# Minimum before maximum in GpSimd's clamp of the weights' upper words

## The chip, the cores and the metric

The kernel runs on one core of a Trainium2 chip. The metric is device time in microseconds (us) of one execution, lower is better; before the change it is the median of three runs. The profile is of one execution, taken by the hardware profiler. Engines are named as in the profile: PE is TensorE's matmul, PEld its weight load, DVE VectorE, ACT ScalarE, POOL GpSimd, SP the engine that issues the DMAs.

## The reference

Linear attention without softmax, an RMS norm for each head, and a feed-forward layer with SiLU:

```python
def _attn_ref(q, k, v, g_norm):            # 8 batches, 8 heads, 576 tokens, 64 per head
    kv = np.einsum('bhsd,bhse->bhde', k, v)
    out = np.einsum('bhsd,bhde->bhse', q, kv)
    rms = np.sqrt(np.mean(out * out, axis=-1, keepdims=True) + 1e-06)
    return (out / rms * g_norm).astype(np.float32)

def _moe_ref(x, w_in, w_out):              # x: 4608 tokens x 512; w_in: 512 x 2048; w_out: 2048 x 512
    h = x @ w_in
    g = h * (1.0 / (1.0 + np.exp(-h)))
    return (g @ w_out).astype(np.float32)
```

The attention's output, with the heads side by side, is x. The two weight matrices arrive as 64-bit floats.

## The kernel before

**Tiles.** The 4608 tokens are nine tiles of 512 (t = 0 to 8), and the 2048 hidden columns are 16 blocks of 128 (f = 0 to 15). The main loop runs over t and inside it over f. One step (t, f) computes the block's hidden values by `products` (line 428) on PE, the gate by `gate` (line 437), and two steps later the block's share of the output by `project` (line 457). Every operand of these matmuls is kept as an upper and a lower part (xh and xl, gh and gl, and the two halves of a weight block), and three products of parts stand for one. `products` therefore has 12 matmuls in a step and `project` 12. The attention of the later batches is spread over the steps by tables of jobs.

**Weights.** A block of w_in (wi0 to wi15) or of w_out (wo0 to wo15) is 128 x 512 numbers of 64 bits. It is turned into float32 parts once, and then stays in SBUF for all nine tiles. So the conversion of nearly all blocks falls into the first tile, t = 0, whose step f prepares the blocks wi of f + 2 and wo of f, with the clamps of one block further. A few blocks come before, in the startup. For each block:

1. `load_block` (line 105): a DMA of 512 KB from the SP queue; upper and lower 32-bit words lie side by side.
2. `magnitude` (line 118): ACT takes the upper words, read as float32, without their sign into the tile `full` (line 126); GpSimd clamps `full` in place to the limits SMALLEST and LARGEST (line 127). For block wi0 alone both are done on VectorE (lines 122 and 127).
3. `bits` (line 131): three bit operations on VectorE (lines 146, 149 and 152) put the float32 together from `full` and the two words.
4. `split_block` (line 157): ACT rounds to the upper part (line 160), GpSimd subtracts to the lower part (line 161).

In the first tile GpSimd also has the subtraction that makes gl (line 443; in the other tiles it is VectorE's), and the one that makes xl from the attention's output (lines 295 and 399).

**Order.** The program is written under a manual schedule: each engine runs its instructions in the order in which the code issues them. In step f of the first tile this is, for GpSimd, the lower parts of the two blocks prepared in the step before (line 161), the clamps of two further blocks (line 127), the subtraction for gl (line 443), and any xl. A block's bits can't be put together before its clamp, its parts not before its bits, and PE's `products` and `project` wait for the parts. The tiles `full` come from a pool of eight buffers shared with other temporaries; gf (line 439) has one buffer. The loads' order is the list ORDER at the top of the file.

Of the kernel before, what the change touches and what calls it, by code (L numbers as in the profile page):

```python
# [12 lines left out]
ALU = mybir.AluOpType  # L13
# [6 lines left out]
SMALLEST = 2.0 ** -15  # L20
LARGEST = 122879.9921875
# [9 lines left out]
def linear_attention_rms_silu_ffn(  # L31
# [51 lines left out]
    for i in range(4):  # L83
        nc.gpsimd.tensor_copy(
            out=both[32 * i:32 * i + 32, 32 * (i ^ 1):32 * (i ^ 1) + 32], in_=ident[32 * i:32 * i + 32, 32 * i:32 * i + 32]
# [24 lines left out]
    def low_high(kind, f):  # L110
        w = words[kind, f].rearrange("p a b -> p (a b)").rearrange("p (n two) -> p n two", two=2)
        return w[:, :, 0], w[:, :, 1]

    def full_tile(kind, f):
        fulls[kind, f] = t = tmp.tile([P, S], F32, name="full", tag="tmp")[:, :NP * P]
        return t

    def magnitude(kind, f, on_vector=False):

        full, high = full_tile(kind, f), low_high(kind, f)[1]  # L120
        if on_vector:
            nc.vector.tensor_scalar(
                out=full.bitcast(I32), in0=high, scalar1=0x7FFFFFFF, scalar2=None, op0=ALU.bitwise_and
            )
        else:
            nc.scalar.activation(out=full, in_=high.bitcast(F32), func=AF.Abs)  # L126
        (nc.vector if on_vector else nc.gpsimd).tensor_scalar(  # L127
            out=full, in0=full, scalar1=SMALLEST, scalar2=LARGEST, op0=ALU.max, op1=ALU.min
        )

    def bits(kind, f):
# [389 lines left out]
    with tc.manual_schedule():  # L521
# [64 lines left out]
        keep_warm(2)  # L586
        p0.copy_kv()
        magnitude("wi", 0, True)
        w("wi0", 1)
        p0.make_out()  # L590
# [18 lines left out]
        p2.copy_kv()  # L609
        n(p1, 2)  # L610
        magnitude("wi", 1)
        p2.make_out()
        n(p1, 4)
# [13 lines left out]
        n(p2, 4)  # L627
        x(p1, 2)
        magnitude("wi", 2)
        n(p3, 2)  # L630
        p2.make_x()
# [114 lines left out]
```

## Time and profile before

| | |
|---|---|
| median of three runs | 904.36 us (904.27 to 904.51) |
| the profiled execution's own time | 904.43 us |
| its span, first to last instruction | 902.7 us |
| instructions in the span | 11085 |
| mean granted clock of TensorE | 0.996 |
| read from and written to HBM | 45.09 MB, 9.44 MB |

The profile's page gives busy times of each engine, and slices of the span in which a digit is the busy share in tenths. A group of instructions reads: line, engine, operation, output <- inputs, shapes, count, then busy us and mean ns of one, then the idle time of the engine just before them, with what ended it. A row of a timeline reads: start, duration, engine and instruction, then in brackets the idle time before it. A row of waits reads: who waited for whom, us in total, how often, the longest.

The chain of work that ended last lies on PE for 84% of the span, almost all of it in lines 432 and 462, the matmuls of `products` and `project`.

### The profile page before, as it was taken

The page shows a single profiled execution, that of the slowest core. Times are in us where ns is not written, and L with a number is a line of the kernel's source. Part 1 is how long each engine was busy: PE and PEld are TensorE (multiplying, and loading weights), DVE is VectorE, ACT ScalarE, POOL GpSimd, SP SyncE. Part 2 cuts the span into 40 slices and gives each one's busy share as a digit, 9 for nine tenths or more (in the row PEclk, how much of TensorE's full clock was granted, in tenths as well). Part 3 has the DMA queues.
Part 4 walks back from the last instruction along what each step waited for, and adds up shares of the span by engine and source line. Part 5 has one row for each costly group of instructions (what it writes and reads, how often), then busy time and mean ns, then how long its engine had stood idle before and what let it go on. Part 6 is the DMA issues. An engine that isn't in the chain of part 4 may idle for free.

```text
span 902.7 us, 11085 instructions
## 1 busy us (share of the span) xinstructions
PE 878.6 (97%) x4472; PEld 717.3 (79%) x4472; DVE 300.5 (33%) x535; ACT 301.8 (33%) x671; POOL 210.0 (23%) x180
## 2 busy tenths in 40 slices
PE   8899879999999999999999999999999999999998
PEld 8677657888888888888888888888888888888887
DVE  4766683323241324232423224232513141111111
ACT  4656443432243224422432234322432232112112
POOL 2999995200111012101120112001210010000000
PEclk9999999999999999999999999999999999999999
DMA  9549101310032003200221014100300010001001
GB/s 333 230 159 366 51 1 44 122 40 1 1 126 80 0 1 126 67 13 1 91 75 40 1 38 128 40 1 1 126 1 1 1 47 1 1 1 48 1 0 47
DMA packets 23971, 55.24 MB, mean 61 GB/s; under 512 B 2800, under 2 KB 3056, under 8 KB 23920
## 3 DMA queue, kind: packets, MB, share of 16 engines
q1 hardware_dynamic: 23920, 54.54, 17.6%
q8 instruction: 35, 0.57, 0.3%
q14 instruction: 16, 0.13, 0.0%
HBM read 45.09 MB, written 9.44 MB: 60 GB/s over the span
## 4 chain that ended last, share of the span: by engine, by line
PE 84%; POOL 0%; ACT 0%; issue 0%; ACTq 0%
PE hp L432 39%; PE acc L462 39%; PE at L222 2%; PE at L260 1%; PE at L261 1%; PE at L259 1%; PE at L462 1%; PE at L409 0%; PE at L408 0%; POOL xl L295 0%; ACT ob L467 0%; ACTq L467 0%
## 5 line engine op out<-in xcount | busy, mean ns | idle before, releaser
L432 PE MATMUL hp<-xh,wi 128*128 128x512 f32 x1144 | 355.3, 392 | 11.0 <-POOL wi L161 11.0
L462 PE MATMUL acc<-wo,gh 128*128 128x512 f32 (+1 forms) x1152 | 357.4, 392 | 0.1
L432 PEld LDWEIGHTS hp<-xh,wi 128*128 128x128 f32 x1144 | 215.0, 188 | 56.6 <-POOL wi L161 13.9
L443 DVE TENSOR_TENSOR gl<-gf,gh 128x512 fp32r<-128x512 f32 x128 | 88.6, 692 | 503.7 <-ACT gf L442 503.7
L462 PEld LDWEIGHTS acc<-wo,gh 128*128 128x128 f32 x1152 | 215.5, 189 | 44.8 <-POOL wo L161 0.3
L441 ACT ACTIVATE gh<-hp 128x512 fp32r<-128x512 f32 x143 | 85.4, 597 | 437.6 <-PE hp L432 437.4
L432 PE MATMUL hp<-xl,wi 128*128 128x512 f32 x572 | 228.2, 399 | 1.5 <-POOL xl L295 1.5
L462 PE MATMUL acc<-wo,gl 128*128 128x512 f32 x576 | 223.3, 388 | 2.4 <-POOL gl L443 2.4
L295 POOL TENSOR_TENSOR xl<-o,xh 128x448 fp32r<-128x448 f32 (+7 forms) x56 | 52.9, 945 | 345.0 <-ACT xh L294 345.0
L462 PEld LDWEIGHTS acc<-wo,gl 128*128 128x128 f32 x576 | 108.6, 189 | 26.6 <-POOL gl L443 2.8
L432 PEld LDWEIGHTS hp<-xl,wi 128*128 128x128 f32 x572 | 107.7, 188 | 24.5 <-POOL xl L295 1.9
L442 ACT ACTIVATE gf<-hp 128x512 f32<-128x512 f32 x143 | 84.8, 593 | 23.0 <-POOL gl L443 22.9
L246 POOL TENSOR_TENSOR ql<-q,qh 128x576 fp32r<-128x576 f32 x24 | 34.2, 1425 | 173.2 <-ACT qh L245 168.2
L127 POOL TENSOR_SCALAR full<-full 128x512 f32<-128x512 f32 x31 | 58.9, 1910 | 0.9 <-ACT full L126 0.9
L286 DVE SCALAR_TENSOR_TENSOR o<-o,gcol,yT 128x448 f32<-128x448 f32 (+7 forms) x56 | 39.0, 696 | 2.0
L265 ACT ACTIVATE sq<-at 128x288 f32<-128x288 f32 x56 | 23.2, 414 | 42.6 <-PE at L261 35.0
L146 DVE TENSOR_SCALAR conv<-full 128x512 int32<-128x512 int32 x32 | 22.2, 694 | 30.7 <-POOL full L127 29.4
L222 PEld LDWEIGHTS at<-v,k 128*64 128x64 f32 (+1 forms) x560 | 20.8, 136 | 14.3 <-issue 8.9
L229 ACT COPY kvm<-at 64x64 f32<-64x64 f32 x56 | 11.5, 205 | 55.5 <-PE at L222 55.2
L222 PE MATMUL at<-v,k 128*64 128x64 f32 (+1 forms) x560 | 26.5, 231 | 1.9 <-ACT o L266 1.9
L279 DVE STREAM_TRANSPOSE yT<-y 128x448 f32<-128x448 f32 (+7 forms) x56 | 26.3, 470 | 0.1
L294 ACT CAST xh<-o 128x448 fp32r<-128x448 f32 (+7 forms) x56 | 24.7, 441 | 0.0
(95 smaller groups left out, 473.7 us busy)
## 6 DMA issues: line engine op xcount, KB each, us to landing
out<-ob SPq DMA_DIRECT2D x35, 256.0 KB, 2.5
wi<-in_moe_w_in SPq DMA_DIRECT2D x16, 512.0 KB, 8.1
wo<-in_moe_w_out SPq DMA_DIRECT2D x16, 512.0 KB, 9.1
k<-in_k SPq DMA_DIRECT2D x28, 288.0 KB, 2.9
v<-in_v SPq DMA_DIRECT2D x28, 288.0 KB, 3.4
q<-in_q SPq DMA_DIRECT2D x28, 288.0 KB, 2.9
early_wo<-in_k SPq DMA_DIRECT2D x2, 288.0 KB, 4.7
early_wi<-in_v SPq DMA_DIRECT2D x2, 288.0 KB, 4.6
```

What stands on the lines that cost most here:

```text
L127: (nc.vector if on_vector else nc.gpsimd).tensor_scalar(out=full, in0=full, scalar1=SMALLEST, scalar2=LARGEST, op0=ALU.max, op1=ALU.min)
L222: nc.tensor.matmul(out=self.kv[h], lhsT=self.k[rows, c, :], rhs=self.v[rows, c, :], start=(r == 0), stop=(r == 4))
L246: nc.gpsimd.tensor_tensor(out=self.ql, in0=self.q, in1=self.qh.bitcast(F32), op=ALU.subtract)
L279: nc.vector.transpose(out=self.yT.rearrange("p (j a) -> p j a", a=32), in_=y[:, a // 32:e // 32].unsqueeze(2).to_broadcast([P, (e - a) // ...
L286: nc.vector.scalar_tensor_tensor(out=self.o[:, a:e], in0=self.o[:, a:e], scalar=gcol, in1=self.yT, op0=ALU.mult, op1=ALU.mult)
L294: nc.scalar.copy(out=th[:, self.c, w], in_=self.o[:, a:e])
L295: nc.gpsimd.tensor_tensor(out=tl[:, self.c, w], in0=self.o[:, a:e], in1=th[:, self.c, w].bitcast(F32), op=ALU.subtract)
L432: nc.tensor.matmul(out=hp[:, :TN], lhsT=w[:, a, fs], rhs=x[:, c, :], start=(c == 0 and i == 0), stop=(c == NP - 1 and i == 2),)
L441: nc.scalar.activation(out=gh, in_=hp[:, :TN], func=AF.Silu)
L442: nc.scalar.activation(out=gf, in_=hp[:, :TN], func=AF.Silu)
L443: (nc.gpsimd if t == 0 else nc.vector).tensor_tensor(out=gl, in0=gf, in1=gh.bitcast(F32), op=ALU.subtract)
L462: nc.tensor.matmul(out=bank, lhsT=g[:, ns], rhs=w[:, a, cs], start=(f == 0 and i == 0), stop=(f == NF - 1 and i == 2))
```

## The change

In the clamp the minimum with LARGEST is now the first operation and the maximum with SMALLEST the second. Line 127 serves both engines, so the one clamp on VectorE (wi0) is changed along with the 31 on GpSimd. The limits are SMALLEST = 2^-15 and LARGEST = 122879.9921875.

```diff
@@ -125,7 +125,7 @@
         else:
             nc.scalar.activation(out=full, in_=high.bitcast(F32), func=AF.Abs)
         (nc.vector if on_vector else nc.gpsimd).tensor_scalar(
-            out=full, in0=full, scalar1=SMALLEST, scalar2=LARGEST, op0=ALU.max, op1=ALU.min
+            out=full, in0=full, scalar1=LARGEST, scalar2=SMALLEST, op0=ALU.min, op1=ALU.max
         )
```

No instruction is added, removed or moved on any engine, and no wait or DMA changes.

## The prediction

> **What bounds the kernel now.** I read the page's busy table and its slices first, then the GpSimd groups, then windows around the place where the changed line runs, and last the waits.
>
> ```profile
> PE 878.6 (97%) x4472; PEld 717.3 (79%) x4472; DVE 300.5 (33%) x535; ACT 301.8 (33%) x671; POOL 210.0 (23%) x180
> ...
> PE   8899879999999999999999999999999999999998
> ...
> POOL 2999995200111012101120112001210010000000
> ...
> L127 POOL TENSOR_SCALAR full<-full 128x512 f32<-128x512 f32 x31 | 58.9, 1910 | 0.9 <-ACT full L126 0.9
> ```
>
> Over the whole span TensorE (PE) is the bound, at 97%, and GpSimd (POOL) has 23%. The averages hide one stage: in slices 2 to 6 (a slice is 902.7/40 = 22.6 us) POOL stands at 9 while PE falls to 7. All 31 changed GpSimd instructions are there; they are 58.9 of POOL's 210.0 us. The changed line also runs once on VectorE, for block wi0. So I look at the first token tile in windows (us from the span's start; then the length, and the busy time and count of each engine):
>
> ```profile
> 34.60:145.00 110.40, 92.33 (x437) 70.56 (x437) 74.47 (x108) 56.40 (x115) 110.40 (x77) 0.97 0.33 121
> ...
> 79.70:87.30 7.60, 7.60 (x50) 6.01 (x49) 5.67 (x9) 4.71 (x12) 7.60 (x7) 1.00 1.03 408
> 87.30:94.80 7.50, 7.50 (x34) 6.12 (x33) 5.55 (x9) 4.74 (x10) 7.50 (x5) 1.00 0.82 311
> ...
> 109.80:117.30 7.50, 5.76 (x25) 4.42 (x24) 6.85 (x17) 3.44 (x6) 7.50 (x6) 1.00 0.01 2
> ...
> 145.00:241.00 96.00, 96.00 (x494) 78.30 (x493) 28.89 (x56) 31.25 (x74) 12.87 (x13) 1.00 0.16 49
> ```
>
> The fifth busy figure is POOL's: from 34.60 to 145.00 us it is busy for 110.40 of 110.40 us, while PE (the first) has 92.33. In the second token tile, 145.00 to 241.00 us, PE is busy all the time and POOL for 12.87 us. So **GpSimd sets the pace of the first tile, for 110.4 us, and TensorE everything after it.** The waits agree:
>
> ```profile
> PE hp L432 <- POOL wi L161: 11.0, 7, 2.8
> ...
> PE acc L462 <- POOL gl L443: 2.4, 1, 2.4
> ...
> PE hp L432 <- POOL xl L295: 1.5, 1, 1.5
> ...
> DVE conv L146 <- POOL full L127: 29.4, 17, 3.8
> ```
>
> PE waits 14.9 us for POOL (11.0 + 2.4 + 1.5) and VectorE waits 29.4 us for the clamp itself. What follows one clamp is queued in order on POOL, and its last item frees the second tile:
>
> ```profile
> 109.84 1.27 POOL L443 TENSOR_TENSOR gl<-gf,gh 128x512 fp32r<-128x512 f32 x1
> 111.08 1.26 POOL L161 TENSOR_TENSOR wi<-full,wi 128x512 fp32r<-128x512 f32 x1
> 112.31 1.28 POOL L161 TENSOR_TENSOR wo<-full,wo 128x512 fp32r<-128x512 f32 x1
> 113.57 3.79 POOL L127 TENSOR_SCALAR full<-full 128x512 f32<-128x512 f32 x2
> 117.33 1.28 POOL L443 TENSOR_TENSOR gl<-gf,gh 128x512 fp32r<-128x512 f32 x1
> ...
> 143.13 1.12 POOL L295 TENSOR_TENSOR xl<-o,xh 128x448 fp32r<-128x448 f32 x1
> ...
> 144.31 0.50 PE L432 MATMUL hp<-xl,wi 128*128 128x512 f32 x1 [1.49 <-POOL xl L295]
> ```
>
> One step of the tile (one f of 16) is gl, wi, wo and two clamps, from 109.84 to 117.33 us: 7.49 us without a gap, of which the two clamps are 3.79. At its end xl ends at 143.13 + 1.12 = 144.25 us and PE starts at 144.31. So each 0.1 us more on a clamp reaches PE undiminished, and each 0.1 us less does until PE itself is the bound.
>
> **The change, part by part.** It moves nothing: instructions, their order on every engine, waits, buffers and DMAs stay. It exchanges two operations and their two constants within each clamp. The lower limit is below the upper one, so the result is the same for every number, and the later instructions see the same data. Only the duration of the 31 GpSimd instructions and of the one on VectorE can change.
>
> *The one on VectorE (wi0).*
>
> ```profile
> L146 DVE TENSOR_SCALAR conv<-full x32: 682/695/697, 8.1 to 138.3; 128x512 int32<-128x512 int32 x32
> L127 POOL TENSOR_SCALAR full<-full x31: 1904/1909/1922, 17.0 to 136.4; 128x512 f32<-128x512 f32 x31
> ...
> L122 DVE TENSOR_SCALAR full<-wi x1: 427/427/427, 7.2 to 7.2; 128x512 int32<-128x512 int32 x1
> L127 DVE TENSOR_SCALAR full<-full x1: 428/428/428, 7.7 to 7.7; 128x512 f32<-128x512 f32 x1
> ```
>
> The columns behind the name are shortest, median and longest in ns. L122 does one operation in 427 ns, L127 two in 428 ns. The second operation costs VectorE nothing, so which is the second cannot matter: 0 taken. The far end would be the slower VectorE form of the same size, 695 - 428 = 0.27 us, once, and as much less on the other side: ±0.03%, under what counts.
>
> *The 31 on GpSimd.* The trace has no clamp with the minimum first, so its price is bounded. What the rows say of the present form: 31 runs lie between 1904 and 1922 ns, over 31 different blocks and 120 us of differing surroundings. So the time depends neither on the values nor on what runs beside it. How much of it is the loop over elements? Two other sizes give a fixed part and a slope:
>
> ```profile
> 155.55 0.46 POOL L295 TENSOR_TENSOR xl<-o,xh 128x128 fp32r<-128x128 f32 x1 [3.67 <-ACT xh L294]
> ...
> L84 POOL COPY both<-ident 32x32 f32<-32x32 f32 x4 | 0.8, 203 | 0.1
> ...
> L82 POOL COPY both<-ident 128x128 f32<-128x128 f32 x1 | 0.3, 280 | 0.0
> ...
> L161 POOL TENSOR_TENSOR wi<-full,wi 128x512 fp32r<-128x512 f32 x16 | 20.4, 1277 | 12.9 <-ACT wi L160 12.9
> ```
>
> A subtraction of 128 columns takes 460 ns and one of 512 columns 1277 ns: 817/384 = 2.13 ns a column and some 188 ns fixed (an estimate from these two rows). The copies give (280 - 203)/96 = 0.80 ns a column. The clamp, with the same fixed part, has (1909 - 188)/512 = 3.36 ns a column: four times a copy, 1.6 times a subtraction, though it reads only one tensor. So its time is in the arithmetic, not in reading or writing. A maximum and a minimum against a constant are mirror images (compare, then choose); taking 1.68 ns for each gives the same sum in either order. **I take no change, 1909 ns.** The near ends are the fast one of a subtraction, 1281 ns (row of line 443 below), and the slow one of two such passes, one for each operation, 2 x 1281 = 2562 ns. The far ends are a copy of this size, 203 + 480 x 0.80 = 587 ns, and two passes as long as today's, 3818 ns.
>
> [...]
>
> How many of the 31 count? POOL's groups between 34.60 and 145.50 us:
>
> ```profile
> L127 POOL TENSOR_SCALAR full<-full 128x512 f32<-128x512 f32 x27 | 51.2, 1909 | 0.0
> ...
> L443 POOL TENSOR_TENSOR gl<-gf,gh 128x512 fp32r<-128x512 f32 x16 | 20.5, 1281 | 0.0
> ```
>
> 27 clamps lie in the stretch without idle time; the four before it, at 17.0 to 31.1 us, have gaps around them. So the time moves by 27 times the change of one clamp, up to 31 times where it gets slower. At 1909 ns again: 27 x 0 = 0. The profiled execution took 904.43 us around a span of 902.7 us, 0.07 above the median of 904.36 of the three runs; I predict 904.4 us.
>
> **The rivals.** The bound for "faster" or "slower" is 0.2%, 1.8 us, about what a measurement of this kernel can tell from no change; over 27 clamps that is 67 ns on one, 3.5% of it.
>
> *First rival, faster: the new order has a better loop, about as quick as a subtraction (1281 ns).* For it: the clamp is 4 times a copy per column, so there is room. Against it: nothing in a row makes the two orders differ. Price: 27 x (1909 - 1281) = 17.0 us. In the windows from 79.70 to 94.80 us PE has no idle time, so their four clamps (2.5 us) may give nothing: 14.5 to 17.0 us, that is 887 to 890 us, likeliest 889. A loop that gains less gives proportionally less, up to 902.
>
> *Second rival, faster: a loop near the copy's (587 ns).* POOL would save 27 x 1.32 = 35.7 us, more than PE can use, and PE becomes the bound of the first tile. Its floor there:
>
> ```profile
> L462 PE MATMUL acc<-wo,gh 128*128 128x512 f32 x112 | 37.0, 413 | 0.1
> L432 PE MATMUL hp<-xh,wi 128*128 128x512 f32 x112 | 36.8, 411 | 11.0 <-POOL wi L161 11.0
> L432 PE MATMUL hp<-xl,wi 128*128 128x512 f32 x56 | 23.4, 418 | 1.5 <-POOL xl L295 1.5
> L462 PE MATMUL acc<-wo,gl 128*128 128x512 f32 x56 | 22.6, 403 | 2.4 <-POOL gl L443 2.4
> ...
> 145.27 2.79 PE acc L462 x12
> ```
>
> The first four rows are the large matmuls of the stretch, 112 + 112 + 56 + 56 = 336. The chain has twelve in 2.79 us, 0.23 us each at full pace (the mean durations overlap). The second tile, with 16 steps of 24, has 384 in 96 us along with its other work; 48 fewer make 96 - 48 x 0.23 = 85 us, against 110.4 now. So at most 25.4 us go, to 879 us; since the weights' DMAs already run at a share of 1.03 (the column before GB/s, the last) from 79.70 to 87.30 us, some waits will be left, and I put it at 879 to 886, likeliest 883. [...]
>
> *Third rival, slower: the present order is the one with the fused loop, and the other falls back to one pass for each operation.* For it: the row shows the present order alone, which may as well be the better of the two. Against it: 3.36 ns a column, four times a copy, doesn't look like a favoured loop. Price: at 2562 ns 27 x 0.653 = 17.6 us, or 922 us; with all 31, 20.2 us and 925. At 3818 ns 27 x 1.909 = 51.5 us, 956 us. It decides from 67 ns a clamp on, since POOL has no idle time to hide it and PE's next matmul waits behind it in every step.
>
> *That the change does nothing* (both orders run the same loop, or the build writes both alike) is my forecast's time, 904.4.
>
> **How the numbers follow.** No change 0.50 (904.4, spread 903.5 to 905.3); first rival 0.20 (887 to 902); second rival 0.12 (879 to 886); third 0.18 (906 to 956). The two orders being mirror images holds the first up; that the clamp lies so far above a copy keeps 0.32 for faster. The range goes from 881 to 912: it leaves out the lowest part of the second rival (0.03) and all of the third but its mildest part (0.13 left out), 0.16 together. The likeliest case alone has 903.5 to 905.3. Faster 0.32, same 0.50, slower 0.18.
>
> **What would show it.** The median of the POOL group of line 127 settles nearly all: at 1904 to 1922 ns my step is right. If it moved, the time should move by 27 times the difference, the step of 7.49 us by twice it, and POOL should stay without idle time up to about 145 us unless the clamp falls below about 0.97 us (25.4/27 = 0.94 less), where PE would have no more waits for POOL. VectorE's clamp should stay at 428 ns in every case. I am wrong if the duration depends on the order, or if the clamp stays and the time moves all the same.

## The result and the profile after

The changed kernel takes 883.64 us (median of 4 runs, 883.59 to 884.16), the kernel before 904.32 us on the same chip. The ratio is 0.9773, with a 95% interval of 0.9756 to 0.979: **20.7 us or 2.3% faster**, where no change was forecast. The profiled execution took 883.63 us, with a span of 881.8 us.

The instructions of line 127 in the changed kernel: count, then shortest, median and longest in ns.

```profile
L127 POOL TENSOR_SCALAR full<-full x31: 604/615/637, 17.4 to 115.0; 128x512 f32<-128x512 f32 x31
...
L127 DVE TENSOR_SCALAR full<-full x1: 428/428/428, 8.6 to 8.6; 128x512 f32<-128x512 f32 x1
```

GpSimd's clamp fell from 1909 to 615 ns; VectorE's stayed at 428 ns to the nanosecond. From the page of the changed kernel, the engines' totals and POOL's slices (now 22.0 us each):

```profile
PE 872.1 (99%) x4472; PEld 715.1 (81%) x4472; DVE 296.6 (34%) x535; ACT 300.9 (34%) x671; POOL 171.9 (19%) x180
...
POOL 2787961101200102001210121011200020000000
```

POOL has 210.0 - 171.9 = 38.1 us less work: 40.2 us from the clamps (58.9 to 18.7 us), and some 2 us back on other instructions that took longer (the 16 subtractions of wo 21.9 us in place of 20.5). The time fell by only about half of that. To see where the rest went, I take the same work in both kernels: from the first matmul of `project` to the first job of the third batch's attention (line 222), 34.70 to 148.00 us before and 33.84 to 127.21 us after. First the row of before, then of after; behind the length stand PE, PEld, DVE, ACT and POOL busy, then PE's granted clock, the DMA share and GB/s:

```profile
34.70:148.00 113.30, 95.31 (x449) 72.71 (x449) 75.63 (x111) 57.38 (x117) 110.80 (x76) 0.97 0.32 118
34.70:49.03 14.33, 10.08 (x42) 6.98 (x44) 8.58 (x13) 9.10 (x18) 14.33 (x10) 0.76 0.06 23
```

```profile
33.84:127.21 93.37, 89.77 (x448) 71.07 (x448) 71.76 (x111) 56.11 (x117) 77.96 (x76) 1.00 0.41 149
33.84:42.78 8.94, 6.98 (x42) 4.92 (x44) 8.24 (x13) 8.36 (x17) 8.94 (x10) 1.00 0.25 99
...
80.00:127.21 47.21, 47.21 (x208) 38.36 (x206) 35.72 (x59) 25.03 (x48) 41.43 (x39) 1.00 0.14 51
```

The stretch is 19.93 us shorter. PE's idle time in it went from 113.30 - 95.31 = 17.99 us to 93.37 - 89.77 = 3.60 us, 14.39 us less. PE's busy time went down by 5.54 us for the same matmuls, and this has two parts. For the first 42 matmuls it fell by 10.08 - 6.98 = 3.10 us: before, the granted clock was 0.50 from 38.1 to 41.5 us and 0.51 from 44.9 to 48.3 us, each time soon after a wait for POOL (2.4 and 1.9 us), and in the changed kernel it is 1.00 throughout. The other 2.44 us lie behind them, at a granted clock of 1.00 in both kernels. Where PE waits in neither kernel the busy time is equal (9.76 us from 80.24 to 90.00 us before, 9.77 us from 72.31 to 82.08 us after), so this part goes with the waits; how was not shown. Idle and busy time together are the 19.93 us; another 0.86 us was won in the startup (34.70 to 33.84 us). From 80.00 to 127.21 us PE has no idle time any more: the bound of the first tile has passed from GpSimd to TensorE.

PE's remaining waits of the first tile, and POOL's groups in the stretch, where it now waits itself:

```profile
PE acc L462 <- POOL gl L443: 1.1, 1, 1.1
PE hp L432 <- POOL wi L161: 0.9, 1, 0.9
PE at L257 <- ACT o L266: 0.8, 1, 0.8
...
PE at L222 <- ACT o L266: 0.8, 1, 0.8
```

```profile
L161 POOL TENSOR_TENSOR wi<-full,wi 128x512 fp32r<-128x512 f32 x13 | 16.8, 1294 | 8.2 <-ACT wi L160 8.2
L127 POOL TENSOR_SCALAR full<-full 128x512 f32<-128x512 f32 x27 | 16.2, 617 | 0.0
```

Of 14.9 us that PE waited for POOL, 2.0 are left. The 27 clamps of the stretch take 16.2 us in place of 51.2, and POOL waits 8.2 us for ScalarE ahead of wi. POOL's idle time in the stretch is now 93.37 - 77.96 = 15.41 us, where it was 113.30 - 110.80 = 2.50 us: a part of what the quicker clamps save is idle time, which TensorE cannot use.

### The profile page after: what moved, and what is told of

Same layout as the page of the kernel before. It is cut to its first block, busy times and chain, and to the rows that moved or that the text cites. A ratio compares the mean times of both kernels' runs of the same rounds, so it can differ in the third digit from the quotient of the medians.

```text
span 881.8 us, 11085 instructions
## 1 busy us (share of the span) xinstructions
PE 872.1 (99%) x4472; PEld 715.1 (81%) x4472; DVE 296.6 (34%) x535; ACT 300.9 (34%) x671; POOL 171.9 (19%) x180
## 4 chain that ended last, share of the span: by engine, by line
PE 97%; DMA 1%; ACT 1%; POOL 1%; SPq 0%; DVE 0%; issue 0%; ACTq 0%; POOLq 0%
PE hp L432 45%; PE acc L462 44%; PE at L222 3%; DMA early_wo<-in_v 1%; PE at L260 1%; PE at L261 1%; PE at L259 1%; PE at L462 1%; PE hp L542 1%; PE at L257 0%; PE hp L222 0%; PE acc L314 0%; PE at L409 0%; PE at L408 0%; PE acc L432 0%; PE acc L327 0%
## 5 line engine op out<-in xcount | busy, mean ns | idle before, releaser
L286 DVE SCALAR_TENSOR_TENSOR o<-o,gcol,yT 128x448 f32<-128x448 f32 (+7 forms) x56 | 35.3, 631 | 2.0
L161 POOL TENSOR_TENSOR wi<-full,wi 128x512 fp32r<-128x512 f32 x16 | 20.6, 1290 | 23.8 <-ACT wi L160 23.8
```

Of the source, the lines that this page charges most:

```text
L286: nc.vector.scalar_tensor_tensor(out=self.o[:, a:e], in0=self.o[:, a:e], scalar=gcol, in1=self.yT, op0=ALU.mult, op1=ALU.mult)
```

## The experiments

Two questions: is the clamp's duration the whole cause, and why does the order set it? All edits are to the changed kernel.

**Other operations on GpSimd (e1).** A scratch tile of 128 x 512 filled with 1.5 is worked on in place once in each of token tiles 2 to 7, by 16 forms of the instruction, each on a line of its own:

```diff
+    probes = [
+        lambda: nc.gpsimd.tensor_scalar(out=probe, in0=probe, scalar1=SMALLEST, scalar2=LARGEST, op0=ALU.max, op1=ALU.min),
+        lambda: nc.gpsimd.tensor_scalar(out=probe, in0=probe, scalar1=LARGEST, scalar2=SMALLEST, op0=ALU.min, op1=ALU.max),
+        lambda: nc.gpsimd.tensor_scalar(out=probe, in0=probe, scalar1=SMALLEST, scalar2=None, op0=ALU.max),
...
+                if 2 <= t < NT - 1 and f < len(probes):
+                    probes[f]()
```

> The changed kernel with 16 extra GpSimd instructions on a scratch tile in each of token tiles 2 to 7, where GpSimd is idle most of the time: pairs of operations, single operations, other constants, half the columns. Every theory expects 1.9 us for maximum then minimum and 0.6 us for minimum then maximum. Theory 'the pair': only maximum then minimum is slow, and single maximum, single minimum and other pairs take about 0.6 us. Rival 'first operation': everything that begins with maximum takes about 1.9 us (also maximum alone, maximum twice, maximum then add). Rival 'second operation': everything that ends in minimum takes 1.9 us (minimum twice, add then minimum). Rival 'constants': with 1.0 and 2.0 in place of the limits the two orders take the same time. Rival 'start-up cost': at 256 columns the two orders still differ by 1.3 us; if the difference is in the loop it is 0.65 us. Time of the kernel: about 884 us, up to 890.

The rows of the lines, in this order: maximum-minimum, minimum-maximum, maximum alone, minimum alone, maximum twice, minimum twice; then (530, 531) the two orders with 1.0 and 2.0; add-multiply (532); maximum-add, add-minimum (534, 535); add-maximum (537); and the two orders at 256 columns (538, 539).

```profile
L524 POOL TENSOR_SCALAR probe<-probe x6: 1910/1916/1917, 211.9 to 691.8; 128x512 f32<-128x512 f32 x6
L525 POOL TENSOR_SCALAR probe<-probe x6: 615/615/615, 226.7 to 693.8; 128x512 f32<-128x512 f32 x6
L526 POOL TENSOR_SCALAR probe<-probe x6: 1484/1486/1493, 231.0 to 711.3; 128x512 f32<-128x512 f32 x6
L527 POOL TENSOR_SCALAR probe<-probe x6: 1492/1492/1941, 239.5 to 714.2; 128x512 f32<-128x512 f32 x6
L528 POOL TENSOR_SCALAR probe<-probe x6: 2101/2207/2375, 241.9 to 719.7; 128x512 f32<-128x512 f32 x6
L529 POOL TENSOR_SCALAR probe<-probe x6: 1932/1932/1932, 252.4 to 725.1; 128x512 f32<-128x512 f32 x6
L530 POOL TENSOR_SCALAR probe<-probe x6: 1922/1922/1923, 254.4 to 727.1; 128x512 f32<-128x512 f32 x6
L531 POOL TENSOR_SCALAR probe<-probe x6: 615/615/798, 265.2 to 729.1; 128x512 f32<-128x512 f32 x6
L532 POOL TENSOR_SCALAR probe<-probe x6: 618/625/625, 265.9 to 730.0; 128x512 f32<-128x512 f32 x6
...
L534 POOL TENSOR_SCALAR probe<-probe x6: 1924/1927/1932, 267.7 to 731.4; 128x512 f32<-128x512 f32 x6
L535 POOL TENSOR_SCALAR probe<-probe x6: 1928/1930/1939, 269.8 to 733.4; 128x512 f32<-128x512 f32 x6
...
L537 POOL TENSOR_SCALAR probe<-probe x6: 1925/2014/2172, 296.9 to 737.5; 128x512 f32<-128x512 f32 x6
L538 POOL TENSOR_SCALAR probe<-probe x6: 1064/1156/1315, 302.4 to 739.5; 128x256 f32<-128x256 f32 x6
L539 POOL TENSOR_SCALAR probe<-probe x6: 392/395/400, 307.8 to 740.6; 128x256 f32<-128x256 f32 x6
```

None of the theories had it right. Not maximum-minimum is the exception, but minimum-maximum: a single maximum takes 1486 ns, more than twice the pair that includes it, and of the other pairs only add-multiply is as quick (multiply-add, line 533, took 619 ns at its shortest but 1011 in the median; in e5, at another place, 618 to 619). The rival of the first operation fails too, since minimum twice takes 1932 ns; that of the second, since add-maximum (line 537) took 1925 ns at its shortest and ends as the quick pair does; and the constants have no part in it (1922 against 615 ns with 1.0 and 2.0). The kernel's time was 883.27 us (one execution). At 256 columns the orders differ by 0.67 us with the shortest runs (1064 and 392 ns), at 512 by 1.30 (1910 and 615): the difference grows with the columns and is not a fixed part. Maximum twice (528) looks slower still, at 2101 to 2375 ns, but its place is one at which VectorE's scaling of the attention's output (line 288 here, 286 in the kernels before and after) runs in each of the six tiles: in the trace of after it starts there at 242.16, 338.24, 434.33, 530.41, 626.50 and 719.56 us. Minimum-add (line 536), where it runs in five of the six (291.55 to 675.36 us), took 1924 to 2172 ns, and in e5 another pair at the place of maximum twice took 2042 to 2377 (line 528), so the excess of maximum twice over 1.93 us comes with its place.

**More forms (e5).** The same kernel with 16 others.

> The changed kernel with 16 other extra GpSimd instructions in token tiles 2 to 7. Theory 'a few pairs have a loop of their own, all else runs in a general loop': a single multiplication or addition takes 1.49 us, as single maximum and minimum did; multiply-add and add-multiply take 0.62 us, subtract-multiply and multiply-subtract perhaps too; multiply twice, add twice, multiply with maximum or minimum take 1.9 us. The minimum-maximum pair takes 0.62 us also with limits that really cut (1.0 and 0.5 on 1.5), and maximum-minimum 1.92 us. Columns: minimum-maximum at 128 about 0.28 us, maximum-minimum at 128 about 0.64 us. Rival 'multiply and add are quick in any form': a single one, and two alike, take 0.6 us.

Multiply alone, add alone, multiply twice, add twice, subtract-multiply (524 to 528); multiply-add, add-multiply, and minimum-maximum with limits that cut (533 to 535); minimum-maximum at 128 columns (537), single maximum at 256 (538), maximum-minimum at 128 (539):

```profile
L524 POOL TENSOR_SCALAR probe<-probe x6: 1498/1500/1509, 212.2 to 692.2; 128x512 f32<-128x512 f32 x6
L525 POOL TENSOR_SCALAR probe<-probe x6: 1495/1497/1506, 226.8 to 693.8; 128x512 f32<-128x512 f32 x6
L526 POOL TENSOR_SCALAR probe<-probe x6: 612/618/623, 231.1 to 711.4; 128x512 f32<-128x512 f32 x6
L527 POOL TENSOR_SCALAR probe<-probe x6: 1935/1936/2380, 239.6 to 714.3; 128x512 f32<-128x512 f32 x6
L528 POOL TENSOR_SCALAR probe<-probe x6: 2042/2214/2377, 242.1 to 719.8; 128x512 f32<-128x512 f32 x6
...
L533 POOL TENSOR_SCALAR probe<-probe x6: 618/619/619, 269.4 to 733.5; 128x512 f32<-128x512 f32 x6
L534 POOL TENSOR_SCALAR probe<-probe x6: 617/618/619, 270.1 to 734.2; 128x512 f32<-128x512 f32 x6
L535 POOL TENSOR_SCALAR probe<-probe x6: 612/613/929, 270.8 to 734.9; 128x512 f32<-128x512 f32 x6
...
L537 POOL TENSOR_SCALAR probe<-probe x6: 293/354/421, 297.1 to 737.9; 128x128 f32<-128x128 f32 x6
L538 POOL TENSOR_SCALAR probe<-probe x6: 841/934/1086, 302.5 to 738.2; 128x256 f32<-128x256 f32 x6
L539 POOL TENSOR_SCALAR probe<-probe x6: 632/634/641, 307.9 to 739.2; 128x128 f32<-128x128 f32 x6
```

The theory holds with one miss: multiply twice is quick as well. Subtract-multiply and multiply-subtract, which it left open, are slow. Quick here are minimum-maximum, multiply-add, add-multiply and multiply twice, at 613 to 619 ns in the median of this run; multiply with minimum, maximum or subtract took 1.93 us or more in each order tried. Everything else follows one pattern: 1.49 us with one operation, some 0.43 us more for the second (line 528, at 2042 to 2377 ns, stands at the place beside VectorE's scaling here too). Maximum-minimum took 634 ns at 128 columns and 1916 at 512 (e1), which is 3.34 ns a column; minimum-maximum 293 (shortest) and 615, which is 0.84 ns. That a few pairs have a loop of their own and all else runs in a general one is what these rows look like; the loops themselves were not seen.

**The clamp made twice (e2).**

```diff
+        for _ in range(1 if on_vector else 2):
+            (nc.vector if on_vector else nc.gpsimd).tensor_scalar(
+                out=full, in0=full, scalar1=LARGEST, scalar2=SMALLEST, op0=ALU.min, op1=ALU.max
+            )
```

> The changed kernel with each GpSimd clamp made twice (the second does nothing more): 1.2 us for a clamp. Theory 'only the clamp's duration counts': GpSimd's work in the first tile is 110.4 - 27 x 0.72 = 91 us, close to the 90 us that the stretch takes now, so the time rises by 2 to 7 us, to 886 to 891 us. Rival 'the order itself has another effect (clock, loads, VectorE)': the minimum still comes first, so the time stays at 883 to 885 us.

891.3 us (890.62 to 891.71). The minimum still comes first, yet more than a third of the gain is gone. In POOL's timeline four clamps, two blocks, hold the engine for 2.56 us, from 62.10 us to the next instruction at 64.66: 1.28 us a block, where 1.2 was expected.

**The clamp made three times (e3).** As e2, with 3.

> The changed kernel with each GpSimd clamp made three times: 1.77 us from the first start to the next instruction, against 1.885 before the change. Theory 'only the clamp's duration counts': GpSimd is the bound of the first tile again and the time returns to 904.3 - 27 x 0.115 = 901 us (899 to 903), with the low TensorE clock between 38 and 49 us back as well. Rival 'the order itself has another effect': clearly below 899 us.

908.43 us (908.36 to 910.1), ratio to before 1.0043 (1.0026 to 1.006): the whole gain is gone, and more. POOL's timeline of e3 and a window of it:

```profile
61.90 3.98 POOL L128 TENSOR_SCALAR full<-full 128x512 f32<-128x512 f32 x6
65.84 1.30 POOL L444 TENSOR_TENSOR gl<-gf,gh 128x512 fp32r<-128x512 f32 x1
```

```profile
43.00:49.00 6.00, 4.31 (x10) 3.44 (x11) 2.65 (x5) 3.57 (x7) 5.75 (x8) 0.53 0.00 0
```

Six clamps occupy 65.84 - 61.90 = 3.94 us, or 1.97 us a block; before the change the two took 117.33 - 113.57 = 3.76 us, or 1.88. So the stand-in was slower than the original by 0.09 us a block, not quicker by 0.115 us as I expected, and 31 x 0.09 = 2.8 of the 4.0 us above before (904.47 us beside these runs) are explained. The low TensorE clock is back as well, at 0.53. The direction and most of the size fit the duration as the only cause; the last 1.2 us stay open. The trace is of the longest of the four executions (910.1 us; the others took 908.4 to 908.5) and shows two further costs: two of GpSimd's subtractions of wo took 1.66 us instead of 1.28, at 131.55 and 138.79 us beside VectorE's scaling (131.09 to 132.08 and 137.95 to 139.30 us), and the mean granted clock was 0.991, where the other three had 0.994.

**No clamp on GpSimd (e4).**

```diff
-        (nc.vector if on_vector else nc.gpsimd).tensor_scalar(
-            out=full, in0=full, scalar1=LARGEST, scalar2=SMALLEST, op0=ALU.min, op1=ALU.max
-        )
+        if on_vector:
+            nc.vector.tensor_scalar(
+                out=full, in0=full, scalar1=LARGEST, scalar2=SMALLEST, op0=ALU.min, op1=ALU.max
+            )
```

> The changed kernel without the 31 clamps on GpSimd (the clamp is left out; the one on VectorE stays). Theory 'TensorE is the bound of the first tile now': 16 us of GpSimd work go and the time moves by 0 to -3 us, 881 to 884 us. Rival 'GpSimd is still the bound': the time falls by most of 27 x 0.59 = 16 us, to 868 to 872 us.

883.27 us (882.79 to 883.82), the changed kernel's time (883.64). Nothing more is to be had from a quicker clamp: TensorE is the bound.

**The clamp as two instructions (e7).**

```diff
+            nc.gpsimd.tensor_scalar(out=full, in0=full, scalar1=SMALLEST, scalar2=None, op0=ALU.max)
+            nc.gpsimd.tensor_scalar(out=full, in0=full, scalar1=LARGEST, scalar2=None, op0=ALU.min)
```

> The changed kernel with each GpSimd clamp as two instructions, the maximum alone and then the minimum alone. By the probes a single operation takes 1.49 us, so with the wait of the second for the first about 3.1 us a block: GpSimd is the bound of the first tile and the time is 904.4 + 27 x (3.1 - 1.9) = 937 us (930 to 942). Rival 'only the pair maximum-minimum is slow in this kernel': two quick ones, 1.3 us a block, about 891 us as with two clamps.

941.2 us (939.63 to 941.46), ratio 1.0399 (1.0382 to 1.0417). Lines 132 and 133 are the maximum and the minimum:

```profile
L132 POOL TENSOR_SCALAR full<-full 128x512 f32<-128x512 f32 x31 | 46.7, 1506 | 0.2 <-ACT full L126 0.2
L133 POOL TENSOR_SCALAR full<-full 128x512 f32<-128x512 f32 x31 | 46.3, 1492 | 2.6
```

The single operations cost in place what they cost on the scratch tile. In POOL's timeline a block's two take 3.03 us from start to start, 1.15 more than the old clamp. The time is 36.6 us above before (904.59 us beside these runs), 31.8 us for each us on one clamp. The startup has its share: the first matmul of `project` starts at 38.20 us instead of 34.70, 3.5 us later, and the stretch that follows is 33.4 us longer (146.74 us), against 27 x 1.15 = 31.1. So on the slow side the four clamps ahead of the stretch count too.

**VectorE's clamp back to maximum first (e6).**

```diff
+            out=full, in0=full, scalar1=SMALLEST if on_vector else LARGEST, scalar2=LARGEST if on_vector else SMALLEST,
+            op0=ALU.max if on_vector else ALU.min, op1=ALU.min if on_vector else ALU.max
```

> The changed kernel with the one clamp on VectorE (block wi0) back to maximum first; the 31 on GpSimd stay with the minimum first. Theory 'VectorE's order is free': 428 ns as in both kernels, time 883.3 to 884.2 us. Rival 'part of the gain is VectorE's': above 884.5 us.

883.81 us (883.25 to 884.07), with 428 ns for the one clamp. VectorE has no part in the gain.

**GpSimd's clamps behind the gate (e8).** The loop over `magnitude` is moved from ahead of the step's matmuls to just behind `gate`.

> The changed kernel with the two clamps of a step issued after the step's gate instead of ahead of it, so that GpSimd subtracts gl before it clamps. TensorE still waits 1.1 us for gl and 0.9 us for a weight block at the start of the first tile. If these waits are what is left there, the time falls by 0.5 to 1.5 us, to 882 to 883 us. If ScalarE's new order (its two gate instructions ahead of the next blocks' magnitudes) delays the clamps by as much, no change: 883.3 to 884.2.

883.63 us (883.44 to 883.68): no change. The first wait for gl fell from 1.1 to 0.5 us, and that for the next weight block grew from 0.9 to 1.6, as the clamp now came later. No version tried beats the changed kernel by more than can be measured.

## Why the prediction was wrong

**What bounds the kernel: right.** GpSimd did set the pace of the first tile. e2, e3 and e7 lengthen nothing but GpSimd's clamps and move the time by 7.7, 24.8 and 57.6 us above the changed kernel's.

**VectorE's clamp at 0: right,** by the row (428 ns) and by e6.

**The step that failed:** "A maximum and a minimum against a constant are mirror images (compare, then choose); taking 1.68 ns for each gives the same sum in either order. I take no change, 1909 ns." The pair in the new order takes 615 ns. The step took the instruction as a sum of two costs that belong to its operations. e1 shows that they don't add up that way: the maximum alone takes 1486 ns, the pair 615. By the step a single operation would take 188 + 512 x 1.68 = 1048 ns; e1 has 1486, and in the slow pairs the second adds only 0.43 us. What has a cost here is the pair in its order, and mirror images can differ. Why the quick pairs are quick stays open.

The rows had spoken against the step: I worked out 3.36 ns a column for the clamp against 0.80 for a copy, and a single-input instruction that runs at a quarter of the copy's pace leaves room for another way to run it. I used that for the rivals and gave the right one 0.12.

**The second rival's price, with PE as the bound: right.** A clamp near a copy's time (587 ns by the two copy rows; 615 measured, 0.84 ns a column) makes PE the bound, at 879 to 886 us, likeliest 883; measured 883.64.

**The floor of TensorE: near.** I had 85 us for the first tile's stretch and allowed for waits. For equal work PE is busy 89.77 us, with 12 more large matmuls in it (the counts of line 462 are 120 and 60 there, not 112 and 56), or 2.8 us; so 87 us, and 3.6 us of waits came on top. That the likeliest figure of 883 is so close has some luck in it, since the working has no sum for the waits.

**The first rival's price, which e2 comes close to testing** (1.28 us a block, where it had 1.281): 887 to 890 us predicted, 891.3 measured. The straight rule gives 904.4 - 27 x (1.88 - 1.28) = 888.2, and 2.5 us were allowed for parts in which PE has no idle time. The rest was not traced in full; in e2 POOL was busy for 85.52 of the 89.40 us from 34.60 to 124.00, with 0.93 us of waiting for ScalarE ahead of the wi at 73.20 us, and its 16 subtractions of wo took 21.1 us instead of 20.5. So POOL did not stay without idle time, as the prediction expected of any clamp above 0.97 us.

**What I had not seen:** the low clock of TensorE, 0.76 between 34.70 and 49.03 us, was in the trace of before and not in my working. It cost PE 3.1 us of busy time there, in a stage where POOL was the bound anyway. In the changed kernel it is gone, and with GpSimd slow again it came back (e3, 0.53).

**Two readings that went too far.** Of the 31 clamps 29 start in slices 2 to 6; the first, at 17.0 us, and the last, at 136.4, lie just outside. And from 31 equal durations I read that a clamp's time does not depend on what runs beside it. In e1 the same maximum-minimum at 256 columns took from 1064 to 1315 ns over its six runs, at a place where VectorE's scaling runs in five of the six tiles (in the trace of after from 302.48 to 686.30 us). Neither changes the sum.

## What to carry to other kernels

On GpSimd, price an instruction by its exact form: order of operations included (1909 against 615 ns here), and don't split or halve a measured cost among its operations. A form whose time per column is several times that of a copy is worth a test of its equivalents (the other order; a neutral second operation, since a single multiplication took 1.50 us and two 0.62), and such a test costs little where the engine is idle, as in tiles 2 to 7 here (883.27 and 883.36 us with the forms of e1 and e5, 883.64 without). And look at an engine with 23% of the span by stage: here it set the time of one, for 110.4 us.

## What the runs showed of the hardware that was not expected

- On GpSimd one operation took longer than a quick pair that includes it, at 128 x 512 float32: 1.49 us for maximum against 0.62 us for minimum-maximum, 1.50 us for multiplication against 0.62 us for two.
- In e7 a GpSimd instruction that works on what the one before it wrote started some 0.11 us later than an independent one: the minimum started 1.57 us after the maximum of its block, and the next block's maximum 1.46 us after that minimum.
- VectorE's scaling of the attention's output (line 286) took longer in some runs beside GpSimd's instructions, and some of GpSimd's took longer beside it. At 128 x 448 it took 0.69 us with POOL idle (before, at 627.88 us). The first row is of before, the others of after, with shortest, median and longest in ns:

```profile
L286 DVE SCALAR_TENSOR_TENSOR o<-o,gcol,yT x56: 284/552/3144, 114.5 to 740.4; 128x448 f32<-128x448 f32 x8, 128x128 f32<-128x128 f32 x8, 128x384 f32<-128x384 f32 x8, 128x192 f32<-128x192 f32 x8
```

```profile
L286 DVE SCALAR_TENSOR_TENSOR o<-o,gcol,yT x56: 283/552/1696, 100.3 to 719.6; 128x448 f32<-128x448 f32 x8, 128x128 f32<-128x128 f32 x8, 128x384 f32<-128x384 f32 x8, 128x192 f32<-128x192 f32 x8
...
L161 POOL TENSOR_TENSOR wo<-full,wo x16: 1274/1299/1685, 32.5 to 122.6; 128x512 fp32r<-128x512 f32 x16
```

Before, when POOL was busy without a gap, the longest of line 286, at 128 x 448 too, took 3.14 us; after, 1.70 us, and three of GpSimd's subtractions took 1.68 to 1.69 us beside it instead of 1.3. Before, none of the subtractions of line 161 was lengthened, though four lay wholly or in part beside the two longest runs of line 286. What decides which of the two engines is held up was not tested.
